# All loads of a DMA-bound kernel in one pinned order on the Pool queue, with a cast by the DMA

## The chip, the cores and the metric

The kernel runs on one core of a Trainium2 chip. The metric is the device time of one execution in microseconds (us), as the median of several executions. A profiled execution of the same program gives the trace; its span is about 2 us shorter than the measured time. An execution counts as fast when it lies within 1.5% of the fastest of the same kernel.

## The reference, cut to what matters

```python
# q, k, v: [8, 8, 576, 64] f32; f: [8, 8, 576]; moe_w_r, moe_w_i: [64, 512, 512] f32; moe_w_ch: [512, 512]
scores = scale * q @ k.T + (cum[:, :, :, None] - cum[:, :, None, :])   # cum: cumsum of log f; causal
x = softmax(scores) @ v                                # -> [8, 576, 512], 64 columns per head
X = rfft(x, axis=1)                                    # the first 64 modes are mixed
Yr = einsum('bmd,mde->bme', Xr, w_r) - einsum('bmd,mde->bme', Xi, w_i)   # and Yi likewise
u = x + irfft(Y)
out = u + maximum(u @ w_ch, 0)
```

The mode weights are 2 x 64 x 512 x 512 x 4 B = 134 MB, and each is used once. q, k and v together are 28 MB. Nothing else that is read is large, so the kernel reads 164 MB and does comparatively little with it.

## The kernel before

Weights stream through a ring of nine tiles, in 64 tiles of 1 MB in bf16 (two loads each, real and imaginary part). They are loaded from the Pool queue, which casts f32 to bf16 on the way. q, k and v of a "pair" (two batches, two heads) are loaded as f32 from the Sync queue into two stage buffers, and an engine casts them.

```python
NRING = 9
STG = 2

def emit_w_load(n):                       # n-th weight tile, first half of the tiles
    wb = wpool.tile([128, 2, MG, D], BF16, tag="wb", name="wb")
    for t, src in enumerate((moe_w_r, moe_w_i)):
        nc.gpsimd.dma_start(wb[:, t, :, :], src[...].rearrange("m p e -> p m e"))
# ... second half: rows of 4 KB instead of 2 KB

QKVst = [[stq.tile([128, 2, NR, Dh], F32, name=f"st{nm}{i}") for nm in "qkv"] for i in range(STG)]

def emit_loads(pr):
    for d, src in zip(QKVst[pr % STG], (k, q, v)):
        nc.sync.dma_start(d[...], bass.AP(...))   # 128 partitions x 2 runs of 2304 B
# ... start: two pairs on Sync, nine weight tiles and the channel weights on Pool
for pr in range(STG):
    emit_loads(pr)
for n in range(NRING):
    emit_w_load(n)
nc.gpsimd.dma_start(wch[:], ...)
# ... emit_transposes: k cast on ScalarE, q and v on VectorE
if which == "k":
    nc.scalar.copy(flat, st[:, :, :, :])
elif which == "q":
    nc.vector.tensor_copy(flat, st[:, :, :, :])
# ... the main loop: 32 attention steps; mode groups start after step 8
for s in range(NS + 1):
    pr, h = s // 2, s % 2
    if h == 0 and pr + STG < NPR:
        emit_loads(pr + STG)
    # ... transposes, scores, softmax, attention x v, DFT
    if s > B:                              # B = 8
        while nmode < (s - B) * NTH // (NS - B):
            emit_modes(nmode)              # uses weight tile nmode and frees its place
            nmode += 1
            next_w()                       # loads tile nmode + 8 into the ring
```

In the trace's names stq is filled from k and stk from q in the kernel before (its list is in the order q, k, v and the loads in the order k, q, v). That is a matter of names only.

The softmax here doesn't subtract the row's maximum and nothing guards it: scores larger than these inputs give would overflow.

## Time and profile before

| | before |
|---|---|
| time, median of 4 runs | 458.83 us |
| profiled span | 457.1 us |
| last weight packet lands | 410.9 us |
| from there to the end of the span | 46.2 us |

The page of the kernel before. The row "DMA" is the busy share of the 16 DMA engines in tenths, in 40 slices of 11.4 us. "GB/s" counts what is written: for a load that casts to bf16, half of what is read. The queues follow (packets, MB, share of the engines' time), then the chain of work that ended last.

```profile
span 457.1 us, 10986 instructions
...
DMA  8999999999999999999999999999999999972677
GB/s 229 275 294 294 294 294 283 275 274 274 274 252 239 276 218 273 215 223 206 207 207 208 211 211 211 211 211 211 211 211 211 211 211 212 212 143 93 219 253 264
...
q0 software_dynamic: 51760, 67.64, 83.8%
q1 hardware_dynamic: 18048, 37.77, 24.0%
...
DMA 88%; PE 6%; ACT 1%; issue 1%; DVE 1%; POOL 1%; DVEq 0%; ACTq 0%; POOLq 0%
```

The DMA engines are busy from the second slice to the 35th, and the chain is 88% DMA. q0 is the Pool queue, q1 the Sync queue. The shares add up to more than 100% because packets on one engine overlap a little: the records show 98 ns on average for a weight packet of 1024 B written, which costs 80.2 ns by the fit below.

The stretches view of the kernel before: the stretch in us, busy time of PE, PE weight load, VectorE, ScalarE and Pool with counts, the granted clock, the DMA share and GB/s. The first stretch has both queues at work, the second only weights with rows of 4 KB.

```profile
20.00:200.00 180.00, 136.28 (x2323) 101.47 (x2321) 128.64 (x344) 135.44 (x188) 32.35 (x43) 0.89 1.16 267
...
260.00:390.00 130.00, 83.98 (x1241) 54.14 (x1242) 26.02 (x66) 26.74 (x47) 36.35 (x52) 0.76 1.12 211
```

In the second stretch 211 GB/s written are about 420 GB/s read (a packet of 4096 B in 156.2 ns on each of 16 engines, by the costs below).

How the cost of one packet was worked out: the packet records of the trace give each packet's queue, size and end. In stretches in which the engines are never short of work, the count of each kind of packet per engine, times its cost, must add up to the length of the stretch. A least-squares fit over stretches of 4 or 5 us gives the costs, and the residual is under 1%.

| packet, kernel before | per engine | cost |
|---|---|---|
| Pool, weights, 2048 B read, 1024 B written | 2080 | 80.2 ns |
| Pool, weights, 4096 B read, 2048 B written | 1024 | 156.2 ns |
| Sync, q/k/v, 2304 B read and written | 768 | 101.4 ns |

The first two rows fix a line of about 4 ns plus 37.1 ns per 1000 B read, by which, as an estimate, 2304 B would cost 90 ns. The third row is 11 ns above it. Cost times count is 405 us of work, and the last packet lands at 410.9 us: 2.7 us are lost at the start, about 3 us at the end, where some engines finish before others, and nothing between.

The issues and the cast of k in the kernel before (issue lines: tile and source, queue, count, KB written, median us from issue to landing; cast line: ns min/median/max, first and last start in us).

```profile
stq<-in_k_dram SPq DMA_DIRECT2D x16, 576.0 KB, 9.2
stk<-in_q_dram SPq DMA_DIRECT2D x16, 576.0 KB, 7.9
stv<-in_v_dram SPq DMA_DIRECT2D x16, 576.0 KB, 8.4
```

```profile
L397 ACT CAST kb<-stq x16: 1129/1160/1300, 15.3 to 203.3; 128x1152 bf16<-128x1152 f32 x16
```

### The profile page before, as it was taken

How to read it: one execution, taken by the hardware profiler on the slowest of the kernel's cores; microseconds unless marked ns; L12 is line 12 of the kernel's file. 1: busy time of each engine (PE TensorE's matmuls, PEld its weight loads, DVE VectorE, ACT ScalarE, POOL GpSimd, SP SyncE). 2: the span in 40 equal slices, each digit the busy share in tenths (PEclk: the TensorE clock that was granted, in tenths of full speed). 3: DMA queues.
4: the chain of work that ended last, by engine and by line, in shares of the span. 5: the costliest groups of instructions: out<-in, count | busy, mean ns of one | idle time of the engine just before them, and what ended most of it. 6: DMA issues, size and time to landing. Idle time of an engine off the chain costs nothing.

```text
span 457.1 us, 10986 instructions
## 1 busy us (share of the span) xinstructions
PE 311.7 (68%) x4704; PEld 213.6 (47%) x4704; DVE 235.6 (52%) x592; ACT 227.8 (50%) x329; POOL 121.1 (26%) x154
## 2 busy tenths in 40 slices
PE   2588877988848476675986499997222257348993
PEld 1355656767626355554765356655211133223441
DVE  5769888988836455565885323222000012105774
ACT  3699999898836536573872133442000012005772
POOL 6111111111112121222323232323223232101884
PEclk9999899999967759787997589999555559557998
DMA  8999999999999999999999999999999999972677
GB/s 229 275 294 294 294 294 283 275 274 274 274 252 239 276 218 273 215 223 206 207 207 208 211 211 211 211 211 211 211 211 211 211 211 212 212 143 93 219 253 264
DMA packets 69937, 106.25 MB, mean 232 GB/s; under 512 B 3264, under 2 KB 36544, under 8 KB 69888
## 3 DMA queue, kind: packets, MB, share of 16 engines
q0 software_dynamic: 51760, 67.64, 83.8%
q1 hardware_dynamic: 18048, 37.77, 24.0%
q8 instruction: 37, 0.61, 0.5%
q10 hardware_dynamic: 80, 0.13, 0.2%
q14 instruction: 12, 0.10, 0.1%
HBM read 163.73 MB, written 9.44 MB: 379 GB/s over the span
## 4 chain that ended last, share of the span: by engine, by line
DMA 88%; PE 6%; ACT 1%; issue 1%; DVE 1%; POOL 1%; DVEq 0%; ACTq 0%; POOLq 0%
DMA wb<-in_moe_w_i_dram 66%; DMA wb<-in_moe_w_r_dram 13%; DMA wch<-in_moe_w_ch_dram 8%; PE pz L723 2%; PE pu L735 2%; PE pz L735 1%; ACT uo L751 1%; PE pu L718 1%; PE pl L698 1%; ACT uo L748 0%; POOL wb L88 0%; DVE uo L752 0%; DVE uo L745 0%; DVEq L804 0%; PE pl L694 0%
## 5 line engine op out<-in xcount | busy, mean ns | idle before, releaser
L131 PE MATMUL A<-XT,wb 128*128 128x16 bf16 x2048 | 72.1, 172 | 98.4 <-DMA wb<-in_moe_w_i_dram 71.8
L473 ACT ACTIVATE E<-ps 128x1024 bf16<-128x1024 f32 (+1 forms) x128 | 104.0, 873 | 26.9 <-PE ps L466 26.0
L131 PEld LDWEIGHTS <-wb 128*128 128x128 bf16 x2048 | 63.3, 99 | 113.7 <-DMA wb<-in_moe_w_i_dram 76.3
L146 DVE TENSOR_TENSOR YT<-A,Yacc 128x128 bf16<-128x128 f32 x24 | 8.8, 368 | 95.9 <-PE A L131 95.9
L466 PE MATMUL ps<-QTs,KT 64*128 64x64 bf16 (+4 forms) x384 | 51.2, 304 | 7.6 <-ACT E L473 6.8
L88 POOL DMA_DIRECT2D wb<-in_moe_w_r_dram x32 | 24.5, 764 | 103.5 <-DMA wb<-in_moe_w_r_dram 34.0
L500 PE MATMUL pav<-va,E 128*128 128x65 bf16 x960 | 48.0, 203 | 2.3 <-DVE x_all L509 1.4
L500 PEld LDWEIGHTS <-E 128*128 128x128 bf16 x960 | 39.8, 104 | 10.8 <-issue 6.4
L88 POOL DMA_DIRECT2D wb<-in_moe_w_i_dram x32 | 24.1, 753 | 71.4 <-DMA wb<-in_moe_w_i_dram 65.0
L488 DVE TENSOR_TENSOR E<-E,trimask 128x256 bf16<-128x256 bf16 (+2 forms) x128 | 38.6, 316 | 7.8 <-ACT E L473 7.4
L641 ACT CAST XW<-pxw 128x512 bf16<-128x512 f32 x40 | 22.6, 586 | 37.9 <-PE pxw L634 37.9
L100 POOL DMA_DIRECT2D wb<-in_moe_w_r_dram x33 | 22.7, 687 | 66.0 <-DMA wb<-in_moe_w_r_dram 37.9
L653 ACT CAST yy<-pyw 128x512 bf16<-128x512 f32 x8 | 4.7, 585 | 70.8 <-PE pyw L646 70.8
L634 PE MATMUL pxw<-wch,yy 128*128 128x512 bf16 x160 | 38.1, 391 | 0.0
L100 POOL DMA_DIRECT2D wb<-in_moe_w_i_dram x33 | 23.0, 697 | 54.6 <-DMA wb<-in_moe_w_i_dram 52.2
L749 POOL TENSOR_TENSOR uo<-uo 64x512 f32<-64x512 f32 (+1 forms) x14 | 25.1, 1806 | 28.9 <-DVE uo L745 26.0
L509 DVE TENSOR_TENSOR x_all<-pav,rcp 128x384 bf16<-128x384 f32 x64 | 31.2, 488 | 0.8
L427 ACT COPY KT<-tp 128x640 bf16<-128x640 bf16 (+1 forms) x32 | 23.0, 755 | 14.9 <-PE tp L414 14.9
L466 PEld LDWEIGHTS <-KT 64*128 64x128 bf16 x384 | 18.0, 96 | 20.8 <-issue 10.8
L542 DVE CAST XT<-px 128x128 bf16<-128x128 f32 x32 | 20.8, 808 | 9.0 <-PE px L534 8.8
L546 ACT ACTIVATE XT<-px 128x64 bf16<-128x64 f32 x32 | 14.6, 467 | 20.1 <-DVE XT L542 17.6
L634 PEld LDWEIGHTS <-yy 128*128 128x128 bf16 x160 | 15.1, 100 | 19.5 <-DVE yy L630 5.9
(102 smaller groups left out, 488.5 us busy)
## 6 DMA issues: line engine op xcount, KB each, us to landing
wb<-in_moe_w_r_dram POOLq DMA_DIRECT2D x63, 512.0 KB, 20.0
wb<-in_moe_w_i_dram POOLq DMA_DIRECT2D x63, 512.0 KB, 20.3
stq<-in_k_dram SPq DMA_DIRECT2D x16, 576.0 KB, 9.2
stk<-in_q_dram SPq DMA_DIRECT2D x16, 576.0 KB, 7.9
stv<-in_v_dram SPq DMA_DIRECT2D x16, 576.0 KB, 8.4
out_dram<-uo SPq DMA_DIRECT2D x16, 512.0 KB, 3.0
out_dram<-uo SPq DMA_DIRECT2D x7, 128.0 KB, 2.4
wch<-in_moe_w_ch_dram POOLq DMA_DIRECT2D x1, 512.0 KB, 38.0
```

What stands on the lines that cost most here:

```text
L88: nc.gpsimd.dma_start(wb[:, t, :, :], src[g * MG : (g + 1) * MG, dc * 128 : (dc + 1) * 128, :].rearrange("m p e -> p m e"),)
L100: nc.gpsimd.dma_start(wb[:, t, ms, :], src[g * M2 : (g + 1) * M2, D // 2 : D, :][ms].rearrange("m (p r) e -> p m (r e)", r=2),)
L131: nc.tensor.matmul(A[:, eb, mi, :], lhsT=wb[:, t, mi, r * D + eb * 128 : r * D + (eb + 1) * 128], rhs=XT3[:, m, c0 : c0 + 2 * B], start=(i ...
L427: nc.scalar.copy(rows(KTs[pr % 2][:, :, 0:S]), tv)
L466: nc.tensor.matmul(ps[:, b, o : o + n], lhsT=KTs[pr % 2][bs, h, jb * 128 : (jb + 1) * 128], rhs=QT[pr][bs, h, jb * 128 + c0 : jb * 128 + c ...
L473: nc.scalar.activation(E[:, :, piece * 512 : piece * 512 + w], ps[:, :, 0:w], ACT.Exp, scale=scale,)
L488: nc.vector.tensor_tensor(dg, dg, tr, ALU.mult)
L500: nc.tensor.matmul(pav[:, i, h, :], lhsT=E[:, h, c : c + 128], rhs=va[:, jb, h, :], start=(jb == 0), stop=(jb == sb),)
L509: nc.vector.tensor_tensor(x_all[:, 2 * bp : 2 * bp + 2, sbs[0] : sbs[0] + n, dc * 128 + hd * Dh : dc * 128 + (hd + 1) * Dh,].rearrange("p ...
L634: nc.tensor.matmul(pxw[:, :], lhsT=xT[:, eb, sb * 128 : (sb + 1) * 128], rhs=wch[:, eb, :], start=(eb == 0), stop=(eb == NDC - 1),)
L641: nc.scalar.copy(XW[:, b, sb, :], pxw[:, :])
L749: nc.gpsimd.tensor_tensor(o_sb, o_sb, u_sb, ALU.add)
```

## The change

The intent: put all loads in one queue, in the order in which they are wanted, so that no second stream disturbs the weights. `tc.keep_in_program_order` pins each load: the scheduler may not move it past another. The pair's k, q, v stand between weight tiles. k and q are cast to bf16 by the DMA, which is meant to make room for a third stage buffer and frees ScalarE of the cast of k. The loads of the first two v stay on the Sync queue.

```diff
-    STG = 2
+    STG = 3
+    def pool_dma(dst, src):
+        tc.keep_in_program_order(nc.gpsimd.dma_start(dst, src))
     ... weight loads: nc.gpsimd.dma_start -> pool_dma
         QKVst = [
-            [stq.tile([128, 2, NR, Dh], F32, name=f"st{nm}{i}") for nm in "qkv"]
+            { nm: stq.tile([128, 2, NR, Dh], F32 if nm == "v" else BF16, name=f"st{nm}{i}")
+              for nm in "kqv" }
     ... emit_loads
-                nc.sync.dma_start(...)
+                if nm == "v" and pr < 2:
+                    nc.sync.dma_start(dst, ap)
+                else:
+                    pool_dma(dst, ap)
     ... start: pair 0, pair 1, weight tiles 0 and 1 (was: all nine and wch)
     ... emit_transposes: k and q are both copied by VectorE, bf16 to bf16
-            if h == 0 and pr + STG < NPR:
-                emit_loads(pr + STG)
+            if h == 0 and pr + STG - 1 < NPR:
+                emit_loads(pr + STG - 1)
+            if s < 10 and nload < min(NRING, 3 + 3 * s // 4):
+                next_w()
+            if s == 10:
+                pool_dma(wch[:], ...)
```

More of the change, by code (lines that the diff above doesn't have):

```diff
@@ L87, in emit_w_load @@
             for t, src in enumerate((moe_w_r, moe_w_i)):
-                nc.gpsimd.dma_start(
+                pool_dma(
                     wb[:, t, :, :],
@@ L99, in emit_w_load @@
                 for t, src in enumerate((moe_w_r, moe_w_i)):
-                    nc.gpsimd.dma_start(
+                    pool_dma(
                         wb[:, t, ms, :],
@@ L183 @@
         QKVst = [
-            [stq.tile([128, 2, NR, Dh], F32, name=f"st{nm}{i}") for nm in "qkv"]
+            {
+                nm: stq.tile(
+                    [128, 2, NR, Dh], F32 if nm == "v" else BF16, name=f"st{nm}{i}"
+                )
+                for nm in "kqv"
+            }
             for i in range(STG)
@@ L195, in emit_loads @@
             dc, bp, _ = steps[2 * pr]
-            for d, src in zip(QKVst[pr % STG], (k, q, v)):
+            for nm, src in (("k", k), ("q", q), ("v", v)):
                 one = src[2 * bp, 2 * dc, :, :]
-                nc.sync.dma_start(
-                    d[:, :, :, :].rearrange("p b r d -> p b (r d)"),
-                    bass.AP(
-                        tensor=one.tensor,
-                        offset=one.offset,
-                        ap=[[NR * Dh, 128], [H * S * Dh, 2], [1, NR * Dh]],
-                    ),
-                )
+                dst = QKVst[pr % STG][nm][:, :, :, :].rearrange("p b r d -> p b (r d)")
+                ap = bass.AP(
+                    tensor=one.tensor,
+                    offset=one.offset,
+                    ap=[[NR * Dh, 128], [H * S * Dh, 2], [1, NR * Dh]],
+                )
+                if nm == "v" and pr < 2:
+                    nc.sync.dma_start(dst, ap)
+                else:
+                    pool_dma(dst, ap)
         used = [0]
@@ L225 @@
         nc.sync.dma_start(ft[:], f.rearrange("b h s -> (b h) s"))
-        for pr in range(STG):
-            emit_loads(pr)
+        emit_loads(0)
         nc.gpsimd.memset(trimask[:, :], 1.0)
@@ L246 @@
         )
+        emit_loads(1)
+        emit_w_load(0)
+        emit_w_load(1)
         s_i = ssb.tile([128, NSB], I32, name="s_i")
-        nc.gpsimd.iota(s_i[:], pattern=[[128, NSB]], base=0, channel_multiplier=1)
+        tc.keep_in_program_order(
+            nc.gpsimd.iota(s_i[:], pattern=[[128, NSB]], base=0, channel_multiplier=1)
+        )
         m_i = ssb.tile([128, NM], I32, name="m_i")
-        nc.gpsimd.iota(m_i[:], pattern=[[1, NM]], base=0, channel_multiplier=0)
-        for n in range(NRING):
-            emit_w_load(n)
-        nc.gpsimd.dma_start(wch[:], moe_w_ch.rearrange("(eb p) e -> p eb e", p=128))
+        tc.keep_in_program_order(
+            nc.gpsimd.iota(m_i[:], pattern=[[1, NM]], base=0, channel_multiplier=0)
+        )
         nc.vector.tensor_copy(ident_f[:, :], ident_bf[:, :])
@@ L392, in emit_transposes @@
             for which in what:
-                st = QKVst[pr % STG]["kqv".index(which)]
+                st = QKVst[pr % STG][which]
+                if which == "q":
+                    QT[pr] = qtp.tile([128, 2, S], BF16, tag="QT", name="QTs")
                 sb = qkb.tile([128, NR, 2, Dh], BF16, tag="cb", name=which + "b")
-                flat = sb[:, :, :, :].rearrange("p r b d -> p b r d")
-                if which == "k":
-                    nc.scalar.copy(flat, st[:, :, :, :])
-                elif which == "q":
-                    nc.vector.tensor_copy(flat, st[:, :, :, :])
-                    QT[pr] = qtp.tile([128, 2, S], BF16, tag="QT", name="QTs")
+                if which != "v":
+                    nc.vector.tensor_copy(
+                        sb[:, :, :, :].rearrange("p r b d -> p b r d"), st[:, :, :, :]
+                    )
                 else:
@@ L548 @@
         NS = len(steps)
-        nload = NRING
+        nload = 2
         nmode = 0
@@ L562 @@
             pr, h = s // 2, s % 2
-            if h == 0 and pr + STG < NPR:
-                emit_loads(pr + STG)
+            if h == 0 and pr + STG - 1 < NPR:
[3 more added lines that the diff above has]
+            if s == 10:
+                pool_dma(wch[:], moe_w_ch.rearrange("(eb p) e -> p eb e", p=128))
             if pr + 1 < NPR:
```

## The prediction

> **What bounds the kernel now.** The DMA engines. The page's DMA row stands at 9 from the second slice to the 35th (400 us of the 457.1 us span), and the chain that ended last is 88% DMA, nearly all weight tiles (wb): one unbroken chain of loads from 3.5 to 411.2 us. The output tail after it takes 45.9 us. No compute engine is over 68% busy. So the time is the DMA work of all loads end to end, plus a tail that the change does not touch.
>
> **What a byte costs.** I fitted packet counts per 5 us in the trace's DMA records (residual under 1%). Per engine a weight packet (2 KB read, cast to 1 KB) costs 80 ns, one of the second half (4 KB to 2 KB) 156 ns, a q/k/v packet on the Sync queue (2304 B, no cast) 101.5 ns. The first two make a line of 4 ns + 37.2 ns per 1000 B *read*, by which 2304 B should cost 89.6 ns: the Sync loads are dear by 12 ns. Weights alone read 420 GB/s (211 written, doubled), the mixed first 200 us 385 to 400. The Trainium skill, "DMA: Bandwidth & Descriptors", section "Where 436 GB/s comes from", puts the ceiling at 435 GB/s; 420 agrees. Its section "Issuing engines are not separate DMA queues" says all queues share the 16 engines, so moving loads to Pool buys no bandwidth by itself. The bytes read stay 163.7 MB; the cast halves only what is written.
>
> **What changes.**
> 1. k and q go to the Pool queue with a cast: 512 packets per engine, 101.5 to 89.6 ns (estimate): -6.1 us, all on the critical path.
> 2. v (14 of 16) moves without a cast: 0 to -2.7 us, by whether the 12 ns belong to the Sync queue or to the uncast write. I take -1.3.
> 3. ACT loses the k cast (16 x 1.16 us); DVE casts both, now from bf16 (0.76 us from f32; I guess 0.4). ACT is about 90% busy in slices 3 to 10, so a pair gets 5 to 8% quicker there. Off the critical path; slack.
> 4. One queue, at most 8 DMAs in flight (each issue waits for an old landing), no second stream to fill gaps. Walking the pinned order with these costs, the DMA engines have work through tile 8 until about 79 us; tile 9 needs mode group 0, which ran at 77 to 78.5 us and should run at 70 to 75 now. A bubble of 0 to 4 us is possible, most likely none. Later a pair costs 18 us of DMA against 13 of compute: the queue stays full.
> 5. Pool issues 46 more DMAs at 0.75 us: 35 us on an engine with room.
>
> **Sum.** Stream end 411.2 - 6.1 - 1.3 - 0.5 (earlier start) + 0.5 (expected bubble) = 404; tail 45.9; the measured time is 1.7 us over the profiled span. Predicted 451 us, range 446 to 457. Two per cent is 449.6 us: faster 0.37, same 0.58, slower 0.05.
>
> **What would show it.** k and q packets at 90 ns effective, a read rate of 405 to 415 GB/s in the first 200 us; last weight landing at 402 to 406 us; the DMA row at 9 throughout; ACT's k cast gone; tail 46 us. If v's packets still cost 101 ns, the 12 ns belonged to the uncast write.
>
> **What would make it wrong.** A hole in the DMA row near 75 to 85 us or at every pair, because Pool waits in order for a stage or weight buffer with everything else behind it (up to 470 us); cast packets of 2304 B costing as much as before (457 us); or Sync packets having slowed the weights in a way my fit hides (larger gain).

## The result

The kernel takes 452.18 us against 458.83 us, medians of four runs each. The ratio is 0.9862, with a 95% interval of 0.9831 to 0.9892: faster by 1.4%, which counts as within 2%. Ratios here are the mean time of one kernel's fast runs over that of the other's of the same rounds, so they are not quite the ratio of the quoted medians.

The page of the kernel after the change:

```profile
span 449.9 us, 10945 instructions
...
DMA  8999999999999999999999999999999999963677
GB/s 204 206 234 233 233 233 233 201 214 228 213 232 221 220 233 216 224 233 206 233 233 211 211 211 211 211 211 211 211 211 211 211 211 211 211 124 106 223 267 247
...
q0 software_dynamic: 62480, 85.34, 102.4%
q1 hardware_dynamic: 5536, 10.63, 6.8%
...
DMA 81%; PE 10%; DVE 2%; issue 2%; ACT 2%; POOL 0%; DVEq 0%; POOLq 0%; ACTq 0%
```

The GB/s of the first half look lower than before, 233 against 294. That is the cast, which halves the bytes written for k and q, and not a slower DMA. The queue's 24.0% on Sync have gone to 6.8%, which is mostly the output. The DMA is still the bound. The chain's PE share has grown to 10%.

The issues after the change, then the copy of k, now by VectorE:

```profile
stv<-in_v_dram POOLq DMA_DIRECT2D x14, 576.0 KB, 15.7
stk<-in_k_dram POOLq DMA_DIRECT2D x16, 288.0 KB, 15.7
stq<-in_q_dram POOLq DMA_DIRECT2D x16, 288.0 KB, 15.6
```

```profile
L410 DVE COPY kb<-stk x16: 442/460/720, 18.8 to 234.4; 128x1152 bf16<-128x1152 bf16 x16
```

A load of k now lands 15.7 us after its issue instead of 9.2, since it stands in line behind weights.

The stretches view around 80 us, first one line of the kernel before, then three after the change, and last the weight-only stage after the change:

```profile
80.00:82.00 2.00, 1.69 (x37) 1.22 (x34) 2.00 (x3) 2.00 (x4) 0.28 (x1) 1.00 1.18 251
```

```profile
60.00:76.00 16.00, 12.08 (x192) 8.69 (x190) 14.69 (x45) 13.77 (x22) 2.24 (x4) 1.00 1.21 228
76.00:80.00 4.00, 3.92 (x86) 3.28 (x86) 3.22 (x10) 2.67 (x6) 1.03 (x2) 1.00 1.12 186
80.00:82.00 2.00, 1.94 (x38) 1.29 (x36) 2.00 (x3) 2.00 (x3) 1.88 (x3) 1.00 0.85 128
```

```profile
260.00:390.00 130.00, 84.82 (x1318) 57.22 (x1326) 30.56 (x76) 29.20 (x52) 36.45 (x52) 0.77 1.12 211
```

Between 78 and 84 us the DMA engines run short: the DMA share falls from 1.21 to 0.85, where it was 1.18 before the change. By the packet costs 1.3 us of DMA time are lost there. This gap is called the hole from here on (the bubble, in the prediction). The weight-only stage is as before, at 211 GB/s. The timeline of Pool shows why (start and length in us, what was issued, and in brackets the idle time before it and what ended that):

```profile
64.44 0.74 POOL L84 DMA_DIRECT2D wb<-in_moe_w_i_dram  x1 [1.75 <-DMA wb<-in_moe_w_r_dram]
78.97 0.74 POOL L84 DMA_DIRECT2D wb<-in_moe_w_r_dram  x1 [13.79 <-PE tp L426]
79.70 0.75 POOL L84 DMA_DIRECT2D wb<-in_moe_w_i_dram  x1
80.44 0.72 POOL L84 DMA_DIRECT2D stk<-in_k_dram  x1
```

After 64.44 us Pool issues nothing for 13.8 us. The next load is weight tile 9, whose ring place is freed by mode group 0, the first use of the weights. Group 0 runs at 75.7 to 78.7 us. The bracket names a transpose that ended at about the same time, but the place in the ring is what the load needs; in v_sync below, the bracket of the same load names the mode group's own matmul (A). Everything behind tile 9, the loads of pair 7 above all, could have gone but for the order.

Where the 7.2 us of the span went:

| | before | after |
|---|---|---|
| DMA work of the weights (and wch) | 327 us | 327 us |
| DMA work of 2304 B runs of q, k, v (736 per engine that change queue) | 74.6 us | 66.2 us |
| lost in the hole at 78 to 84 us | 0 | 1.3 us |
| last weight packet lands | 410.9 us | 402.9 us |
| from there to the end | 46.2 us | 47.0 us |

The second row is 736 x 101.4 ns and 736 x 90.0 ns. The cost after the change is the mean over cast and uncast runs, since their costs are hard to separate in that kernel. 8.4 us saved less 1.3 us is 7.1 us, and the landing moved by 8.0 us; the missing 0.9 us are lost less at the start and the end, and were not pursued. The end after the last weight was between 45.6 and 47.5 us in the twelve experiments as well, without an order to it.

### The profile page after: what moved, and what is told of

It reads as the page before. It is cut to its first block, busy times and chain, and to the rows that moved or that the text cites. A ratio compares the mean times of both kernels' runs of the same rounds, so it can differ in the third digit from the quotient of the medians.

```text
span 449.9 us, 10945 instructions
## 1 busy us (share of the span) xinstructions
PE 317.4 (71%) x4688; PEld 218.9 (49%) x4704; DVE 239.0 (53%) x608; ACT 212.6 (47%) x313; POOL 154.6 (34%) x200
## 4 chain that ended last, share of the span: by engine, by line
DMA 81%; PE 10%; DVE 2%; issue 2%; ACT 2%; POOL 0%; DVEq 0%; POOLq 0%; ACTq 0%
DMA wb<-in_moe_w_i_dram 42%; DMA stk<-in_k_dram 18%; DMA stq<-in_q_dram 11%; DMA wb<-in_moe_w_r_dram 7%; DMA stv<-in_v_dram 3%; PE pz L739 2%; PE pu L751 2%; PE pz L751 1%; PE A L134 1%; PE tp L426 1%; ACT uo L767 1%; PE pav L512 1%; PE ps L478 1%; PE pu L734 1%; PE pl L714 1%
## 5 line engine op out<-in xcount | busy, mean ns | idle before, releaser
L134 PEld LDWEIGHTS <-wb 128*128 128x128 bf16 x2048 | 64.3, 100 | 64.3 <-DMA wb<-in_moe_w_i_dram 32.5
L478 PE MATMUL ps<-QTs,KT 64*128 64x64 bf16 (+4 forms) x384 | 56.8, 313 | 10.3 <-ACT E L485 9.5
L426 PE MATMUL tp<-ident_bf,kb 128*128 128x128 bf16 x144 | 16.3, 270 | 30.0 <-DVE kb L410 29.5
L650 PE MATMUL pxw<-wch,yy 128*128 128x512 bf16 x152 | 35.4, 380 | 1.3 <-issue 1.1
L426 PEld LDWEIGHTS <-kb 128*128 128x128 bf16 x144 | 11.7, 121 | 33.7 <-DVE kb L410 30.8
L443 ACT COPY VT<-tp 128x640 bf16<-128x640 bf16 (+1 forms) x32 | 22.5, 754 | 11.0 <-PE tp L426 10.7
L410 DVE COPY kb<-stk 128x1152 bf16<-128x1152 bf16 x16 | 7.9, 495 | 34.2 <-DMA stk<-in_k_dram 34.1
L441 DVE COPY QTs<-tp 128x640 bf16<-128x640 bf16 (+1 forms) x32 | 23.2, 766 | 5.0 <-PE tp L426 4.1
## 6 DMA issues: line engine op xcount, KB each, us to landing
stv<-in_v_dram POOLq DMA_DIRECT2D x14, 576.0 KB, 15.7
stk<-in_k_dram POOLq DMA_DIRECT2D x16, 288.0 KB, 15.7
```

Source lines behind the costliest of these rows:

```text
L134: nc.tensor.matmul(A[:, eb, mi, :], lhsT=wb[:, t, mi, r * D + eb * 128 : r * D + (eb + 1) * 128], rhs=XT3[:, m, c0 : c0 + 2 * B], start=(i ...
L426: nc.tensor.transpose(tp[:, r - r0, :, :].rearrange("c h p -> c (h p)"), sb[:, r, :, :].rearrange("p b d -> p (b d)"), ident_bf[:, :],)
L441: nc.vector.tensor_copy(rows(QT[pr][:, :, :]), tv)
L478: nc.tensor.matmul(ps[:, b, o : o + n], lhsT=KTs[pr % 2][bs, h, jb * 128 : (jb + 1) * 128], rhs=QT[pr][bs, h, jb * 128 + c0 : jb * 128 + c ...
L650: nc.tensor.matmul(pxw[:, :], lhsT=xT[:, eb, sb * 128 : (sb + 1) * 128], rhs=wch[:, eb, :], start=(eb == 0), stop=(eb == NDC - 1),)
```

## The experiments

Theories. *Packet theory*: what pays is that q/k/v packets cost fewer ns of DMA engine time. *Order theory*: the pinned order with weights loaded as wanted pays. *Compute theory*: relieving ScalarE pays. Within the packet theory it was open whether the cast, the longer packets, or leaving the Sync queue makes the packets cheap.

### order_only: the new order, the old loads

```diff
 from the change:  STG = 3 -> 2, stage tiles all F32, lead of two pairs kept
-                if nm == "v" and pr < 2:
-                    nc.sync.dma_start(dst, ap)
-                else:
-                    pool_dma(dst, ap)
+                nc.sync.dma_start(dst, ap)
```

> The change's order of weight loads and its VectorE casts, but q, k and v all go on the Sync queue in f32 with two stage buffers, as before. Packet theory: DMA work is back at 405 us, so 458 to 460 us. Order theory (pinned weights, loaded as they are needed, pay): 452 to 454 us.

Measured: 459.21 us, ratio to before 1.0008 (0.9992 to 1.0025). The queues of its page:

```profile
q0 software_dynamic: 51760, 67.64, 83.7%
q1 hardware_dynamic: 18048, 37.77, 24.0%
```

They are those of the kernel before, and the fit gives 101.6 ns for a Sync packet. The order alone, and with it VectorE's casts in place of ScalarE's, is worth nothing. The order theory falls as an account of the gain.

### front: the new queue, the old order

```diff
-        emit_w_load(0)
-        emit_w_load(1)
+        for n in range(NRING):
+            emit_w_load(n)
-        nload = 2
+        nload = NRING
```

> All on the Pool queue with the cast, but the nine ring tiles of weights stand in front of the third pair, as in the kernel before. Order theory and packet theory agree that the order is then needed: weights and the first two pairs keep the DMA busy to about 57 us, the third pair lands only at about 60 us, attention starts 30 us late and the ring is full till the first mode group, so the DMA engines run dry for about 20 us: 465 to 475 us. If the order does not matter: 452 us.

Measured: 484.42 us, ratio 1.0559 (1.0541 to 1.0576), worse than expected. One line of its stretches view:

```profile
86.00:112.00 26.00, 20.43 (x338) 15.12 (x337) 23.23 (x67) 21.66 (x35) 0.40 (x1) 1.00 0.01 2
```

For 26 us the DMA engines do nothing (share 0.01): the ring is full, the first mode group comes only at 108.4 us, and the loads of later pairs stand behind the weights that wait. Short stretches before it bring the loss to 34 us. So the order earns nothing, but one queue can't do without it. I had expected 20 us because I took attention to catch up sooner.

### v_sync: v back on the Sync queue

```diff
-                if nm == "v" and pr < 2:
+                if nm == "v":
```

> All 16 v loads stay on the Sync queue, else as the change. Packet theory (the gain is DMA engine time of the q/k/v packets): v packets cost 101.5 ns per 2304 B again instead of 84.5, so 224 packets per engine x 17 ns = 3.8 us are lost: 456.0 us, stream end near 406.7. Order theory (one pinned queue is what pays, since a second queue disturbs it): most of the 6.6 us are lost, 457 to 459. Compute theory (the gain is ACT's relief from the k cast): no change, 452.

Measured: 457.01 us, ratio 0.9954 (0.9939 to 0.9969). By time alone this lies where the order theory had it, but the trace divides it. v packets cost 102.2 ns and the cast packets of k and q, now apart, 89.9 ns (by the length of the stretches the fit moves between 102 and 105 ns, and between 89 and 90). So 224 x (102.2 - 90.0) = 2.7 us go to v's packets. The hole is 4.1 us instead of 1.3, as the first mode group came only at 81.8 us. The last weight packet lands 5.9 us later, of which these two are 5.5. Pool waited 20.7 us for tile 9:

```profile
86.17 0.74 POOL L84 DMA_DIRECT2D wb<-in_moe_w_r_dram  x1 [20.68 <-PE A L134]
```

My 84.5 ns for v in the change, and so 3.8 us, came from a fit that could not tell v from k and q well: such fits of the change and of its variants with uncast v put v at 83 to 88 ns and the cast packets at 91 to 92, while v_sync and kq_f32, where the kinds stand apart, give 90 ns for both. Only the sum, 66.2 us, is firm. Why the first mode group came later was not pursued.

### stg2 and kq_f32: without the third buffer, and without the cast

```diff
 stg2, from the change:
-    STG = 3
+    STG = 2
-            if h == 0 and pr + STG - 1 < NPR:
-                emit_loads(pr + STG - 1)
+            if h == 0 and pr + 2 < NPR:
+                emit_loads(pr + 2)
 kq_f32, from stg2:
-                    [128, 2, NR, Dh], F32 if nm == "v" else BF16, name=f"st{nm}{i}"
+                    [128, 2, NR, Dh], F32, name=f"st{nm}{i}"
```

> The change with two stage buffers in place of three, the same order of loads on the Pool queue. If the third buffer matters: Pool waits for the casts of the pair before with all weights behind it, DMA idle of 0.5 us or more at each pair up to step 10, 455 to 465 us. If Pool's lead over the compute engines is set by the 8 DMAs in flight anyway: 452 to 453 us.

> As stg2, but k and q stay f32 on the Pool queue, without a cast[...]. If the cast by the DMA is what makes k and q cheap: packets back at about 101 ns, +6 us on stg2. If leaving the Sync queue and merging to 4608 B does it: 84.5 ns per 2304 B against 90.5 with the cast, 512 x 6 = 3.1 us less than stg2 in DMA work, time 2 to 3 us under stg2 unless VectorE's dearer casts (0.76 against 0.46 us) delay the first mode group.

Measured: stg2 452.29 us, ratio 0.9852 (0.9838 to 0.9867). The third stage buffer is worth nothing here. kq_f32 takes 454.44 us, ratio 0.9895 (0.9880 to 0.9909), 2.1 us more than stg2 and not less.

The DMA work is the same in both, 392.5 against 392.8 us by the fits (each leaves out the few Sync loads at the start). An uncast run of 2304 B costs 89.7 ns (179.3 ns for a packet of two), against 89.9 ns for one that is cast. So the cast by the DMA saves no DMA time that shows (0.3 us in 392), and neither of my expectations held. What the cast saves is on VectorE: its copy of k takes 752 ns from f32 and 460 ns from bf16. The first mode group starts at 78.0 us instead of 76.0, most likely for that reason, and the hole grows from 1.6 to 2.5 us. Its stretches view:

```profile
80.00:84.00 4.00, 3.92 (x81) 2.90 (x79) 3.71 (x8) 3.28 (x5) 3.06 (x5) 1.00 0.54 82
```

Small holes before 60 us bring 0.6 us more. The last weight packet lands 1.6 us later than in stg2, of which the holes are 1.5: the cast pays by way of the holes.

### v_pad and v_split: is it the longer packets?

```diff
 v_pad:   stage tile of v with 32 bytes between its two batches
+                else stq.tile([128, 2 * NR * Dh + 8], F32, name=f"st{nm}{i}")
 v_split: each v load as two, one per batch
+                if nm == "v" and pr >= 2:
+                    for bb in range(2):
+                        pool_dma(dst[:, bb, :], ...)
```

> v on the Pool queue without a cast as in the change, but its stage tile has 32 bytes between the two batches, so that the two 2304 B runs can no longer be one packet of 4608 B. If the Sync queue's packets were dear because of their queue: 2304 B packets cost about 89.6 ns, 448 per engine (halves of 14 loads) lose 224 x 5 ns = 1.2 us: 453.3 us. If they were dear because a write without a cast costs more: 101.5 ns, 456 us. If the merging does nothing: 84.5 ns, 452.2 us.

> Each v load on the Pool queue is two loads, one per batch, so that no packet can be longer than 2304 B. Queue theory (the 12 ns belonged to the Sync queue): 2304 B packets without a cast cost about 90 ns, DMA work as in the change to 1 us, near 452 us. Merge theory (uncast loads got cheap on the Pool queue because packets are 4608 B there): above 95 ns, up to 101.5, and 1.2 to 2.6 us more.

Both missed their aim. v_pad: 451.99 us, ratio 0.9856 (0.9831 to 0.9881), and its packets are 4608 B as before the edit. v_split (one run): 452.88 us, and though the issues doubled, the packet records still show 1792 packets of 4608 B for v:

```profile
stv<-in_v_dram POOLq DMA_DIRECT2D x28, 288.0 KB, 14.1
```

The Pool queue puts two uncast runs in one packet, also with a gap between the batches and also when each load has one run per partition; which two runs share a packet the records do not say. So whether length by itself matters stays open. That cast runs (one per packet) and uncast runs (two per packet) cost the same 90 ns leaves little room for it, unless two effects cancel. v_pad serves as a repeat of the change: 451.99 against 452.18 us.

### hw_alone: Sync packets with no other queue active

```diff
 from kq_f32, ahead of the first loads:
+        for pr in (1, 0):
+            for nm, src in (("v", v), ("q", q), ("k", k)):
+                nc.sync.dma_start(QKVst[pr][nm][...], ...)
```

> kq_f32 with the first two pairs' q, k and v loaded once more at the start, on the Sync queue, before anything is on the Pool queue (the result is the same; the time is worse by about 10 us and is not the question). Six loads are 96 packets of 2304 B per engine with no other queue active. If Sync queue packets are dear in themselves: about 101.5 ns each, 9.7 us from first to last. If they are dear only because the engines go to and fro between two queues: about 90 ns, 8.6 us.

Measured, one look, 462.53 us. Pool's first load waits for these, and the first Pool packet moves at 12.1 us. The stretch before it:

```profile
4.00:12.00 8.00, 2.63 (x16) 2.08 (x16) 5.36 (x14) 2.60 (x5) 3.06 (x4) 1.00 1.05 400
```

Uncast loads run at 400 GB/s, which is 86.8 packets per engine in 8 us, or 92.1 ns each. Beside the Pool queue they cost 101.4 ns, by which 2304 B x 16 / 101.4 ns is 364 GB/s. Some 9 of the 11 ns are therefore not the Sync queue's own, if this one look holds; they arise when the engines have both queues to serve. The 92.1 ns are for packets of one run, so they also leave at most some 2 ns to the packets' length. The Trainium skill, "DMA: Bandwidth & Descriptors", section "Queues, rings and completion order", says that each engine goes round robin between the queues with work, packet by packet. That fits, but it states no cost for the turn, and no run shows the turn itself.

### k_on_act: is it the relief of ScalarE?

```diff
-                    nc.vector.tensor_copy(
+                    (nc.scalar.copy if which == "k" else nc.vector.tensor_copy)(
```

> The copy of k into interleaved order goes back from VectorE to ScalarE (now bf16 to bf16), else as the change. Packet theory: ScalarE is off the critical path but for the first mode group, 452 to 453 us (bubble at most 1 us longer), DMA work unchanged. Compute theory (ScalarE's relief made the gain): back to 457 to 459 us.

Measured: 454.63 us, ratio 0.9900 (0.9880 to 0.9921). DMA work is unchanged. The first mode group comes at 78.1 us and the hole is 2.9 us instead of 1.3:

```profile
80.00:82.00 2.00, 1.86 (x32) 1.30 (x29) 2.00 (x6) 1.80 (x3) 1.84 (x3) 1.00 0.32 31
```

Most of the gain stays, so the compute theory falls as the main account. With ScalarE's 1.15 us per copy (no quicker from bf16 than from f32, 1.16 us) the median is 2.4 us longer. The two profiled runs differ by 1.5 us (453.45 against 451.98 us), which the hole's 1.6 us cover; I had allowed it 1 us.

### wch_early, best, unpinned: closing the hole

```diff
 wch_early: load of wch in front of the weight tile of step 8, not at step 10
 best: wch_early, and
-            if h == 0 and pr + STG - 1 < NPR:
-                emit_loads(pr + STG - 1)
+            if s == 0:
+                emit_loads(2)
+            if h == 1 and pr + 3 < NPR:
+                emit_loads(pr + 3)
 unpinned, from the change:
-        tc.keep_in_program_order(nc.gpsimd.dma_start(dst, src))
+        nc.gpsimd.dma_start(dst, src)
```

> The load of the channel weights (2.6 us of DMA time) moves from step 10 to before the weight tile of step 8, ahead of the tile that waits for the first mode group. Bubble theory (1.3 us of DMA time lost at 76 to 88 us because that tile stands at the head of the queue with everything behind it): bubble gone, 450.9 us, ratio to the change 0.997. If the lost DMA time is given back elsewhere or the first mode group is just as much later: 452.2 us.

> The change, with the channel weights ahead of the weight tile of step 8 (as wch_early) and each pair's q, k and v issued one step earlier, so that the loads of pair 7 stand ahead of the weight tile that waits for the first mode group. Bubble theory: 2.6 + 4.3 us more DMA work stands before that tile, so the 1.3 us hole at 76 to 88 us is gone: no 2 us stretch short of DMA work by more than 0.1 us between 20 and 390 us, stream end near 401.5, 450.5 to 451 us. If the hole was not on the path: 452.2 us.

> The same calls in the same order without the pin, so that the scheduler may move a load past another; the built program differs from the change in a few places from step 9 on (loads of a pair move past weight tiles). If the pin itself is worth time: 453 us or more. If only the order in which the calls are made matters: 452 us, perhaps less, as the pair's loads there move ahead of a waiting weight tile.

| kernel | time | ratio to before (95%) | hole at 76 to 88 us | last weight packet |
|---|---|---|---|---|
| the change | 452.18 us | 0.9862 (0.9831 to 0.9892) | 1.3 us | 402.9 us |
| wch_early | 451.19 us | 0.9834 (0.9813 to 0.9854) | 0.5 us | 402.9 us |
| best | 451.01 us | 0.9827 (0.9813 to 0.9842) | none | 402.3 us |
| unpinned | 451.33 us | 0.9830 (0.9814 to 0.9847) | none | 402.3 us |

The profiled run of wch_early was its slowest (452.41 us), so its row joins a median to a slower execution. The stretches view of best, to be set against the change's:

```profile
76.00:80.00 4.00, 3.90 (x90) 3.33 (x87) 3.23 (x10) 2.76 (x5) 0.51 (x1) 1.00 1.24 206
80.00:82.00 2.00, 1.96 (x36) 1.38 (x35) 2.00 (x4) 2.00 (x3) 1.00 (x2) 1.00 1.25 206
```

The DMA share stays at 1.24 where it fell to 0.85. The hole is gone, yet the last packet lands only 0.6 us earlier: in the last 6 us of the stream, where the supply of work runs out, best's engines are short of work for 0.7 us more than the change's. An inference, not shown: an engine that lags uses the hole to catch up, so a hole costs less than its length. best has the lowest median, 1.2 us under the change's, with wch_early and unpinned within 0.3 us of it. Its interval overlaps the change's, and the last packet of its profiled run lands only 0.6 us earlier, so that closing the hole pays is not proved. Without the pin the scheduler moves the loads of pair 7 past the waiting tile by itself. The pin earns nothing here; whether it costs anything is not clear of the noise.

## Why the prediction was right

The time (452.18 for 451) and the main mechanism held: the loads' DMA work is the path, and k, q and v got cheaper there. That the two times lie so close is partly luck. By the prediction's own count, which sets the end of the stream 0.3 us later than this document does, the stream ended 0.8 us sooner than forecast (403.2 for 404) and the tail took 0.8 us longer (46.7 for 45.9); within the stream, too much gain forecast from the start and too little hole stood against too little gain from v. Point by point:

- *DMA-bound, the saving is packet time on the path*: right. order_only, without the cheaper packets, has none of the gain.
- *k and q, -6.1 us*: 512 x (101.4 - 89.9) = 5.9 us. The size was right and part of the reason wrong. I tied it to the move "with a cast"; kq_f32 shows the same 90 ns without a cast. The sentence that moving loads to Pool buys nothing by itself failed with it: leaving the Sync queue is what made these packets 11 ns cheaper.
- *v, 0 to -2.7 us, I take -1.3*: 224 x (102.2 - 90.0) = 2.7 us. The term was mis-sized by half: the 11 ns belonged to the Sync queue beside the Pool queue, not to the uncast write.
- *ScalarE freed, attention 5 to 8% quicker*: wrong. The first mode group ran at 75.7 to 78.7 us, no sooner done than before (76.7 to 78.5) and not at 70 to 75. From 20 to 76 us ScalarE's busy time fell from 52.3 to 48.1 us of 56, while VectorE's, at 47.0, rose to 48.4 (lines below). It was not for want of loads: VectorE waited 34 us for k in its stage tiles, but all of it after 78 us. What held the pace before that is not shown.
- *A bubble of 0 to 4 us near 79 us, expected 0.5*: 1.3 us, in that place and for that reason.
- *Stream end 404, tail 45.9 us*: 403.2 and 46.7 us, as said above. The start came no earlier, against 0.5 us expected.
- *A read rate of 405 to 415 GB/s in the first 200 us*: by the packet records, 407 GB/s from 20 to 200 us, the hole included (392 before the change), and 400 with the first 20 us. By the packet costs q, k and v go at 410 GB/s (2304 B x 16 / 90.0 ns) and the weights there at 408.

The stretches view from 20 to 76 us, before and then after the change (VectorE is the third busy time, ScalarE the fourth):

```profile
20.00:76.00 56.00, 45.10 (x599) 31.72 (x598) 47.04 (x121) 52.34 (x73) 7.17 (x9) 0.97 1.14 289
```

```profile
20.00:76.00 56.00, 45.73 (x608) 30.88 (x606) 48.42 (x127) 48.08 (x71) 17.23 (x24) 1.00 1.21 234
```

VectorE's wait is this line of the change's waits over the whole span (engine, what it waited for, us in total, times, longest); in the same view of 0 to 78 us it has no line for a load:

```profile
DVE kb L410 <- DMA stk<-in_k_dram: 34.1, 9, 5.6
```

The Trainium skill, "DMA: Bandwidth & Descriptors", section "Issuing engines are not separate DMA queues", says loads from all queues share the engines. The runs agree, and add that sharing was not free: two active queues cost this kernel some 7 us (an estimate: 736 packets at the 9 ns of hw_alone). Its section "Where 436 GB/s comes from" gives 435 GB/s as the ceiling of the fabric at the SBUF; the weight-only stage read 420 GB/s before and after, so little was left to gain there. The same section holds that about 358 GB/s, a core's share of the HBM, binds for loads from HBM; the 420 GB/s measured here, on the one core in use, are above that, and the measurement decides.

## What to carry to other kernels

In a kernel bound by its DMA engines, count the work in packets: fit a cost to each kind, and a change of queue or shape can be priced before it is made. A plain load on a second queue beside a busy one may cost more than the same bytes on the busy queue, but a single queue then stops wherever its head waits, so put loads that wait for nothing in front of the one that waits for compute. Take pinned orders, extra buffers and casts apart before crediting them: here the queue earned the time, and the cast earned only its cheaper copy afterwards.

## What the Trainium skill lacked or had wrong

- "DMA: Bandwidth & Descriptors", section "Queues, rings and completion order", gives the round robin between queues but no cost: a Sync packet of 2304 B cost 92.1 ns alone (one look) and 101.4 ns beside a busy Pool queue, some 7 us over the 736 packets that changed queue here.
- The same page, "Issuing engine by pattern", calls the sync and scalar path generally faster. For uncast loads beside a busy Pool queue it was the dearer one: 101.4 ns on Sync against 89.7 ns on Pool.
- The same page does not say whether a load that casts costs by bytes read or written. Here it was by bytes read: 89.9 ns cast to half the bytes, 89.7 ns uncast.
- The same page, "SWDGE vs HWDGE vs iDMA", gives a packet of preferably at most 4096 B. Uncast runs of 2304 B on the Pool queue were recorded two to a packet, 4608 B, also when each load had one run per partition.
